# Pooled attention and two MLPs on one core: block 1's attention steps two intervals later, keys of heads 5 to 7 pooled on VectorE, the last product token tile by token tile

## The chip, the core and the metric

One NeuronCore of a Trainium2 chip runs the whole program. The metric is device time in microseconds (us) of one launch. The engines are TensorE (PE, with its weight loads PEld), VectorE (DVE), ScalarE (ACT), GpSimd (POOL) and SyncE (SP), whose queue issues nearly all DMAs. Each engine takes its instructions strictly in the order in which the program wrote them and waits on semaphores for the others, so an instruction that waits holds up everything behind it on its engine.

## The reference

```python
def _attn_ref(q, k, v):            # 8 x 8 heads, 576 tokens, head_dim 64
    k_p = k.reshape(B, H, 72, 8, D).mean(axis=3)     # keys and values pooled by 8
    v_p = v.reshape(B, H, 72, 8, D).mean(axis=3)
    scores = scale * np.matmul(q, k_p.transpose(0, 1, 3, 2))
    attn = softmax(scores)
    return np.matmul(attn, v_p)
...
x = attn_out.transpose(0, 2, 1, 3).reshape(4608, 512)
h = x @ w_in;  x = (h * clip(h + 3, 0, 6) / 6) @ w_out           # MLP 1, d_ff 2048
g = x @ w_gate;  out = (silu(g) * (x @ w_val)) @ w_out2           # MLP 2, d_ff 1536
```

The weights arrive as float64 words and are turned into float32 on the chip. All products are made to float32 accuracy from two halves (a high part and a rest), so each product is three matmuls.

## The kernel before

**Attention.** The 4608 tokens are cut into 9 blocks of 512. Heads are taken in pairs ("head" in the code is such a pair; heads 0 to 3 are batch 0, 4 to 7 batch 1). A *unit* is a piece of one head pair's tokens: block 0 has units 0 to 7, block 1 units 8 to 19. Each unit goes through steps with one-letter names: S (scores on PE, then the row maximum on DVE, L453 and L459), X (exponentials on ACT, L476), N (reciprocal of the row sum on DVE, L491 and L492), M (scaling on POOL, L496), E (split of a tail, L503 and L506), T (transposes on PE, L513 and L517), U and L (copy and rest of the transposed tile, ACT L526, DVE L533), V (product with the values on PE, L539 to L542), W and Y (result into the tile x, ACT L550, DVE L554). For each head there are steps for keys (RK and K) and values (R0, R1, R), and for each segment of queries a step P, which on DVE is the transposition L440 of a loaded tile q_in.

**The order.** Two tables, `when_startup` for the units of block 0 and `when` for all others, give each step of unit i an interval (i plus a lag) and a rank in it; all steps are sorted by these into one list. The steps up to the last Y of block 0 run before any MLP work. The rest of the list is dealt out evenly over the MLP's loop, counted by the large steps S, T and V, so that block j+1's attention runs beside block j's MLP 1.

**Keys.** Step RK sums 8 keys per row on DVE (`reduce_k`, two reductions L370), and K then transposes the sum on PE with one matmul (L389). For heads in `pe_pooled` there is no RK: K lets PE add the 8 rows with 16 small matmuls (L393), which the profile shows as 32.

**MLP 1 in block 0.** For each of 16 slices f there is a product h (12 matmuls, L561, needs all of x), an activation (ACT L583, DVE L585), a split, and two slices later a product y (12 matmuls). In block 0 the same loop also turns the weights from float64 into float32, two tiles per f: load into a buffer wstg (3 buffers, L108 on SP), rescale (ACT L120), join (DVE L126, L129), high part (ACT L169), rest (DVE L177). Six such conversions are steps C of the startup. The load of a new tile waits on SP for the join that frees its buffer.

**MLP 2** runs in 6 passes after the last block; its last part, `down2` with n = 6, makes three token tiles of 128 rows in three PSUM banks, chunk by chunk over the inner dimension, and `evac` adds them to the output tile o12 (DVE) and stores it.

The key step, the point where the two ways part:

```python
if what == "RK":
    if i not in pe_pooled:
        reduce_k(*heads[i])
        next_k(i)
elif what == "K":
    transpose_k(*heads[i])
```

Of the kernel before, what the change touches and what calls it, by code (L numbers as in the profile page):

```python
# [12 lines left out]
ALU = mybir.AluOpType  # L13
# [10 lines left out]
def kernel(  # L24
# [27 lines left out]
    nc = tc.nc  # L52
    P = 128
# [34 lines left out]
    M = 384  # L88
    NG = NT // (2 * M)
    NPAIR = F2 // 2  # L90
    PT = M // P
# [489 lines left out]
    def act1(ps):  # L581
        t = t_p.tile([P, N], F32, tag="t", name="t")
        nc.scalar.activation(out=t, in_=ps, func=ACTF.Relu, bias=three)  # L583
        g = t_p.tile([P, N], F32, tag="g32", name="g32")
        nc.vector.scalar_tensor_tensor(out=g, in0=t, scalar=6.0, in1=ps, op0=ALU.min, op1=ALU.mult)  # L585
        return g
# [27 lines left out]
    CH = 2  # L614
    l2 = {}
    xc, ys, gf, gc, wr = {}, {}, {}, {}, {}
# [46 lines left out]
    def bank():  # L663
        return l2["ps"].tile([P, 512], F32, tag="b", name="b")

    def mm3x(ps, w, x, first, last):
        for n, (wh, xh) in enumerate(((0, 0), (0, 1), (1, 0))):
            nc.tensor.matmul(out=ps, lhsT=w(wh), rhs=x(xh), start=first and n == 0, stop=last and n == 2)  # L668
# [4 lines left out]
    def up2(p, u):  # L673


        f, m = u
        add = lambda dst, a, b: nc.vector.tensor_tensor(out=dst, in0=a, in1=b, op=ALU.add)  # L677
        for what, wa, xb in UP:
            b = bank()[:, :M]
            w, x = wr.pop(("up", u, A7[wa])), xc[p, xb]  # L680
            for k in range(2):
                mm3x(b, lambda a: w[:, a, k], lambda a: x[:, a, k], k == 0, k == 1)
            if what == "P1":
                c11 = tmp(f"c11{m}")
                nc.scalar.copy(out=c11, in_=b)  # L685
            elif what == "P6":
                c21 = tmp(f"c21{m}")
                add(c21, c11, b)
            elif what == "P5":
                c12 = tmp(f"c12{m}")  # L690
                add(c12, c21, b)
            elif what == "P2":
                add(c11, c11, b)
            elif what == "P4":
                add(c21, c21, b)
            elif what == "P7":
                c22 = tmp(f"c22{m}")
                add(c22, c12, b)
                add(c21, c21, b)
            else:  # L700
                add(c12, c12, b)
        return {"11": c11, "22": c22, "21": c21, "12": c12}
# [6 lines left out]
    def gate2(c):  # L709
        g = {}  # L710
        for q in ("11", "22", "21", "12"):
            g[q] = tmp("s" + q)
            nc.scalar.activation(out=g[q], in_=c[q], func=ACTF.Sigmoid)  # L713
        for q in ("11", "22", "21", "12"):
            nc.gpsimd.tensor_tensor(out=g[q], in0=g[q], in1=c[q], op=ALU.mult)  # L715
        return g
# [18 lines left out]
    def down2(p, n):  # L735
        what = DN[n][0]
        b = dn_b[what] = [bank()[:, :2 * P] for i in range(PT)]
        for c in range(NPAIR // CH):
            g = gc.pop((p, n, c))
            for t in range(PT):  # L740
                for k in range(CH):
                    w = wr["dn", n, CH * c + k]
                    mm3x(b[t], lambda a: g[:, a, k, t * P:(t + 1) * P], lambda a: w[:, a],
                         c == 0 and k == 0, c == NPAIR // CH - 1 and k == CH - 1)

    o_t = {}

    def evac(p, n):

        what = DN[n][0]  # L750
        b = dn_b[what]

        def out_tile(tag):
            o_t[tag] = l2["o"].tile([P, PT, 2 * P], F32, tag=tag, name=tag)
            return o_t[tag]

        def add(dst, a):
            for t in range(PT):
                nc.vector.tensor_tensor(out=dst[:, t], in0=a[:, t], in1=b[t], op=ALU.add)

        def copy(dst):
            for t in range(PT):
                nc.scalar.copy(out=dst[:, t], in_=b[t])

        def store(tag, r, c):
            t0 = 2 * M * p + M * r
            nc.sync.dma_start(
                out=out[t0:t0 + M, 2 * P * c:2 * P * (c + 1)].rearrange("(t p) d -> p t d", p=P),
                in_=o_t[tag],
            )  # L770

        if what == "P1":
            copy(out_tile("o12"))
        elif what == "P4":
            copy(out_tile("o21"))
        elif what == "P2":
            add(out_tile("o11"), o_t["o12"])
            store("o11", 0, 0)
        elif what == "P6":
            add(o_t["o12"], o_t["o12"])  # L780
            nc.vector.tensor_tensor(out=o_t["o21"], in0=o_t["o21"], in1=o_t["o12"], op=ALU.add)
        elif what == "P5":
            add(o_t["o12"], o_t["o12"])
        elif what == "P7":
            add(o_t["o21"], o_t["o21"])
            add(out_tile("o22"), o_t["o12"])
            store("o21", 1, 0)
            store("o22", 1, 1)
        else:
            add(o_t["o12"], o_t["o12"])  # L790
            store("o12", 0, 1)

# [8 lines left out]
    for j in range(NB):  # L801
        t0 = j * N
        while t0 < (j + 1) * N:
            b, s0 = t0 // S, t0 % S
            n = min(S - s0, (j + 1) * N - t0)
# [14 lines left out]
        unit_end.append(len(units))  # L820
    NU = len(units)
    early_units = set(units[:unit_end[1]])
    pe_pooled = {5, 6, 7}

# [15 lines left out]
    }  # L840
    events = []
    for i in range(NU):
        startup_unit = i < unit_end[0]
        lag = dict(when_startup if startup_unit else when)
        if 0 <= i - unit_end[0] < NE:
            lag["E"] = (1, 22)
        stages = [(what, i) for what in "SXNMETULVWY"]
        if 2 <= i < 8:
            stages.append(("C", i))
        if i in first_in_seg:  # L850
            stages.append(("P", first_in_seg[i]))
        if i in first_in_head:
            stages += [(what, first_in_head[i]) for what in ("RK", "K", "R0", "R1", "R")]
        events += [(i + lag[st[0]][0], lag[st[0]][1], st[1], st) for st in stages]
# [119 lines left out]
    with tc.manual_schedule():  # L974
# [6 lines left out]
            out=vmask[:, 0], in_=vmask[:, 0], compare_op=ALU.is_ge, fill=0.0,  # L981
# [3 lines left out]
            out=vmask[:, 1], in_=vmask[:, 1], compare_op=ALU.is_ge, fill=0.0,  # L985
# [45 lines left out]
        for n, (j, f) in enumerate(seq1):  # L1031
# [13 lines left out]
            g = act1(hp)  # L1045
# [28 lines left out]
        for p in range(NG):  # L1074
            for n, (f, m) in enumerate(units2):
                c = up2(p, (f, m))
                load_next()
                if m == 0:
                    g = gate2(c)
                else:  # L1080
                    val2(p, f, g, c)
                    if f % CH == CH - 1:
                        split_gc(p, 0, f // CH, nc.vector)
                        split_gc(p, 1, f // CH, nc.vector)
                        if f + 1 < NPAIR:
                            sums_g(p, ("S1", "S3", "S2"), f + 1 - CH, f + 1)
                if n == 2 and p + 1 < NG:
                    load_y(p + 1, y_pool)
            NC = NPAIR // CH
            for n in range(7):  # L1090
                down2(p, n)
                load_next()
                if n + 2 < 7:
                    for c in range(NC):
                        split_gc(p, n + 2, c, nc.vector)
                if n == 0:
                    sums_g(p, ("S1", "S3", "S2"), NPAIR - CH, NPAIR)
                    for a in range(0, NPAIR, NPAIR // 2):
                        sums_g(p, ("S4",), a, a + NPAIR // 2)
                evac(p, n)  # L1100
                if p + 1 < NG:
                    x_step(p + 1, n, nc.vector, nc.vector)
# [29 lines left out]
```

## Time and profile before

| what | value |
|---|---|
| median of 3 runs | 1784.87 us (1782.77 to 1784.95) |
| profiled execution | 1784.89 us, span of its instructions 1783.1 us |
| mean granted TensorE clock | 0.989 of full speed |
| PE busy | 1741.5 us (98%) |
| DVE, ACT, POOL busy | 1208.7 us, 687.5 us, 632.7 us |

The span is the time from the first to the last instruction; 1.8 us of the execution lie around it. Times in the trace count from the span's start. A granted clock of 1.00 is the higher of TensorE's two levels (2.4 GHz), 0.50 the lower (1.2 GHz). A row of a timeline gives start, length, engine, line, operation, output and input, and in brackets how long the engine had been idle and what ended that.

### The profile page before, as it was taken

How to read it: one execution, taken by the hardware profiler on the slowest of the kernel's cores; microseconds unless marked ns; L12 is line 12 of the kernel's file. 1: busy time of each engine (PE TensorE's matmuls, PEld its weight loads, DVE VectorE, ACT ScalarE, POOL GpSimd, SP SyncE). 2: the span in 40 equal slices, each digit the busy share in tenths (PEclk: the TensorE clock that was granted, in tenths of full speed). 3: DMA queues.
4: the chain of work that ended last, by engine and by line, in shares of the span. 5: the costliest groups of instructions: out<-in, count | busy, mean ns of one | idle time of the engine just before them, and what ended most of it. 6: DMA issues, size and time to landing. Idle time of an engine off the chain costs nothing.

```text
span 1783.1 us, 28056 instructions
## 1 busy us (share of the span) xinstructions
PE 1741.5 (98%) x9945; PEld 1575.7 (88%) x9945; DVE 1208.7 (68%) x2216; ACT 687.5 (39%) x1580; POOL 632.7 (35%) x769
## 2 busy tenths in 40 slices
PE   5899999999999999999999999999999999999999
PEld 4677788888888878878888999999999999999999
DVE  7887677768577666765522468568668568668666
ACT  6565444434444434444323225124224224224222
POOL 5343342414315133251112351361461460550550
PEclk8899999999999999999999999999999999999999
DMA  7765557666657666565354677977977877878776
GB/s 173 224 221 168 177 166 243 211 203 194 206 182 208 219 187 203 169 182 197 113 207 179 238 255 249 329 249 255 328 246 258 316 247 269 314 245 279 272 245 213
DMA packets 196315, 402.93 MB, mean 226 GB/s; under 512 B 85840, under 2 KB 121680, under 8 KB 185424
## 3 DMA queue, kind: packets, MB, share of 16 engines
q1 hardware_dynamic: 192528, 396.16, 67.8%
q10 hardware_dynamic: 3648, 4.98, 0.8%
q8 instruction: 79, 1.29, 0.3%
q14 instruction: 60, 0.49, 0.1%
HBM read 340.79 MB, written 60.29 MB: 225 GB/s over the span
## 4 chain that ended last, share of the span: by engine, by line
PE 89%; DVE 4%; ACT 2%; DMA 2%; issue 1%; POOL 1%; SPq 0%; DVEq 0%; POOLq 0%; ACTq 0%
PE b L668 44%; PE y L561 20%; PE h L561 19%; PE pss L453 2%; PE pst L513 1%; PE pst L517 1%; DMA qs<-in_q_dram 1%; DVE fly L177 1%; ACT e L476 1%; DVE w L129 1%; DVE w L126 1%; PE psv L542 1%; DMA vts<-in_v_dram 1%; PE psv L540 0%; PE psv L541 0%
## 5 line engine op out<-in xcount | busy, mean ns | idle before, releaser
L668 PE MATMUL b<-xc,wr 128*128 128x384 f32 x3024 | 525.2, 334 | 0.0
L668 PEld LDWEIGHTS b<-xc,wr 128*128 128x128 f32 x3024 | 524.0, 188 | 0.1
L561 PE MATMUL y<-g,fly 128*128 128x512 f32 x1728 | 431.8, 399 | 1.6 <-ACT yo L602 1.6
L561 PE MATMUL h<-x,wu 128*128 128x512 f32 x1728 | 431.9, 399 | 0.0
L677 DVE TENSOR_TENSOR c<-c,b 128x384 f32<-128x384 f32 x504 | 265.0, 552 | 178.6 <-PE b L668 151.4
L561 PEld LDWEIGHTS y<-g,fly 128*128 128x128 f32 x1728 | 319.4, 190 | 66.3 <-ACT yo L602 2.0
L561 PEld LDWEIGHTS h<-x,wu 128*128 128x128 f32 x1728 | 319.4, 190 | 64.4 <-issue 0.4
L715 POOL TENSOR_TENSOR s<-s,c 128x384 f32<-128x384 f32 x144 | 142.5, 1015 | 400.4 <-ACT s L713 400.4
L668 PE MATMUL b<-wr,gc 128*128 128x256 f32 x2268 | 265.6, 279 | 0.0
L668 PEld LDWEIGHTS b<-wr,gc 128*128 128x128 f32 x2268 | 265.4, 188 | 0.0
L496 POOL TENSOR_TENSOR e<-e,sm 96x288 f32<-96x288 f32 (+3 forms) x85 | 70.5, 830 | 466.4 <-DVE sm L492 331.0
L722 POOL TENSOR_TENSOR gf<-s,c 128x384 f32<-128x384 f32 x144 | 168.3, 1194 | 67.0 <-DVE c L677 66.2
L134 ACT CAST gc<-gf 128x768 fp32r<-128x768 f32 x126 | 105.6, 838 | 187.0 <-POOL gf L722 99.8
L713 ACT ACTIVATE s<-c 128x384 f32<-128x384 f32 x144 | 73.5, 526 | 202.4 <-DVE c L677 201.2
L135 DVE TENSOR_TENSOR gc<-gf,gc 128x768 fp32r<-128x768 f32 x126 | 133.7, 1093 | 15.7 <-ACT gc L134 13.9
L135 DVE TENSOR_TENSOR g<-g,g 128x512 fp32r<-128x512 f32 x128 | 93.9, 733 | 67.4 <-ACT g L134 66.8
L585 DVE SCALAR_TENSOR_TENSOR g<-t,h 128x512 f32<-128x512 f32 x144 | 97.6, 678 | 60.4 <-ACT t L583 57.0
L134 ACT CAST g<-g 128x512 fp32r<-128x512 f32 x144 | 88.7, 616 | 68.5 <-PE y L561 47.6
L583 ACT ACTIVATE t<-h,three 128x512 f32<-128x512 f32 x144 | 98.5, 684 | 38.9 <-PE h L561 38.5
L483 ACT ACTIVATE e<-e 96x288 f32<-96x288 f32 (+3 forms) x76 | 31.4, 413 | 153.2 <-DVE e L480 151.5
L685 ACT COPY c<-b 128x384 f32<-128x384 f32 x72 | 34.0, 472 | 144.9 <-PE b L668 144.9
L205 DVE TENSOR_TENSOR gf<-gf 128x768 f32<-128x768 f32 (+1 forms) x66 | 66.9, 1029 | 12.2 <-POOL gf L722 10.9
(105 smaller groups left out, 1635.3 us busy)
## 6 DMA issues: line engine op xcount, KB each, us to landing
wr<-sup SPq DMA_DIRECT2D x72, 1024.0 KB
fly<-w1d SPq DMA_DIRECT2D x128, 512.0 KB
wr<-sdn SPq DMA_DIRECT2D x84, 768.0 KB
wr<-sup SPq DMA_DIRECT2D x72, 768.0 KB
sup<-s SPq DMA_DIRECT2D x12, 1792.0 KB
sdn<-s SPq DMA_DIRECT2D x6, 1792.0 KB
ystg<-y SPq DMA_DIRECT2D x24, 384.0 KB
out_dram<-o SPq DMA_DIRECT2D x24, 384.0 KB
```

The costliest lines, as they stand in the source:

```text
L134: nc.scalar.copy(out=hi, in_=src)
L135: lo_engine.tensor_tensor(out=lo, in0=src, in1=f32(hi), op=ALU.subtract)
L205: eng.tensor_tensor(out=v(what), in0=v(a), in1=v(b), op=op)
L496: nc.gpsimd.tensor_tensor(out=e3, in0=e3, in1=sm.to_broadcast(list(e3.shape)), op=ALU.mult)
L561: nc.tensor.matmul(out=ps, lhsT=w(kt, wh), rhs=x(kt, xh), start=first and n == 0, stop=last and n == 3 * len(kts) - 1,)
L583: nc.scalar.activation(out=t, in_=ps, func=ACTF.Relu, bias=three)
L585: nc.vector.scalar_tensor_tensor(out=g, in0=t, scalar=6.0, in1=ps, op0=ALU.min, op1=ALU.mult)
L668: nc.tensor.matmul(out=ps, lhsT=w(wh), rhs=x(xh), start=first and n == 0, stop=last and n == 2)
L677: add = lambda dst, a, b: nc.vector.tensor_tensor(out=dst, in0=a, in1=b, op=ALU.add)
L713: nc.scalar.activation(out=g[q], in_=c[q], func=ACTF.Sigmoid)
L715: nc.gpsimd.tensor_tensor(out=g[q], in0=g[q], in1=c[q], op=ALU.mult)
L722: nc.gpsimd.tensor_tensor(out=gf[p][:, GP[TURN[q]], f], in0=g[q], in1=c[q], op=ALU.mult)
```

## The change

Three edits. `HOLD = 2` adds two intervals to every step of units 8 and up, while block 0's units stay; since all later units move alike, only their order against the startup changes. `pe_pooled` is emptied, so heads 5, 6 and 7 get the step RK on DVE and the short K on PE like all others. In the last pass the last product runs token tile by token tile, and each tile is added and stored as it is done.

```diff
     def down2(p, n):
...
+        order = [(c, t) for c in range(NC) for t in range(PT)]
+        if (p, n) == (NG - 1, 6):
+
+            order.sort(key=lambda ct: ct[1])
+        for c, t in order:
+            g = gc[p, n, c]
...
-            add(o_t["o12"], o_t["o12"])
-            store("o12", 0, 1)
+            for t in range(PT):
+                o = o_t["o12"][:, t]
+                nc.vector.tensor_tensor(out=o, in0=o, in1=b[t], op=ALU.add)
+                if p == NG - 1:
+                    t0 = 2 * M * p + P * t
+                    nc.sync.dma_start(out=out[t0:t0 + P, 2 * P:], in_=o)
+            if p < NG - 1:
+                store("o12", 0, 1)
...
-    pe_pooled = {5, 6, 7}
+    pe_pooled = set()
...
+    HOLD = 2
...
+        if not startup_unit:
+            lag = {what: (a + HOLD, rank) for what, (a, rank) in lag.items()}
```

What this does to the order shows at three places. On PE, the first product h before; the steps ahead of it are units 6 to 8's transposes, unit 10's scores (`kbd_130`), then the value products of unit 8 (64 columns) and unit 7 (256 columns):

```order
L513 MATMUL pst<-ident,es 128x64
L517 MATMUL pst<-ident,et_142 96x64
L453 MATMUL pss<-kbd_130,qT 64x144
L539 MATMUL psv<-aT,vst_132 128x64
L540 MATMUL psv<-aT,vst_132 128x64
L541 MATMUL psv<-aT,vst_132 128x64
L542 MATMUL psv<-aTt,vtl_136 128x64
L539 MATMUL psv<-aT,vst_135 128x256
L540 MATMUL psv<-aT,vst_135 128x256
L541 MATMUL psv<-aT,vst_135 128x256
L542 MATMUL psv<-aTt,vtl_139 128x256
L561 MATMUL h<-x,wu 128x512 x12
```

The same place of the change:

```order
L453 MATMUL pss<-kbd_128,qT 64x144
L539 MATMUL psv<-aT,vst_135 128x256
L540 MATMUL psv<-aT,vst_135 128x256
L541 MATMUL psv<-aT,vst_135 128x256
L542 MATMUL psv<-aTt,vtl_139 128x256
L561 MATMUL h<-x,wu 128x512 x12
L453 MATMUL pss<-kbd_129,qT 64x144
L513 MATMUL pst<-ident,es 128x64
L517 MATMUL pst<-ident,et_142 96x64
L453 MATMUL pss<-kbd_130,qT 64x144
```

Scores of units 9 and 10 and transposes and value product of unit 8 have moved behind the first h; only unit 8's scores stay ahead of it. From the scores of unit 20 on, PE's order is the same in both.

On SP, the loads of the startup's last intervals before: the fourth and fifth weight tile (L108), values, and between them the queries of segments 6 and 7 (L361, four pieces each):

```order
L108 DMA wstg<-in_moe_w_in_dram 128x4x256
L361 DMA q_in<-in_q_dram 32x2x32 x4
L108 DMA wstg<-in_moe_w_out_dram 128x1024
L314 DMA vts<-in_v_dram 16x512 x3
L308 DMA v_in<-in_v_dram 72x512
L309 DMA v_in<-in_v_dram 56x512
L308 DMA v_in<-in_v_dram 72x512
L309 DMA v_in<-in_v_dram 56x512
L361 DMA q_in<-in_q_dram 32x2x32 x4
L108 DMA wstg<-in_moe_w_in_dram 128x4x256
```

The same place of the change:

```order
L108 DMA wstg<-in_moe_w_in_dram 128x4x256
L108 DMA wstg<-in_moe_w_out_dram 128x1024
L314 DMA vts<-in_v_dram 16x512 x3
L308 DMA v_in<-in_v_dram 72x512
L309 DMA v_in<-in_v_dram 56x512
L308 DMA v_in<-in_v_dram 72x512
L309 DMA v_in<-in_v_dram 56x512
L108 DMA wstg<-in_moe_w_in_dram 128x4x256
L108 DMA wstg<-in_moe_w_out_dram 128x1024
L361 DMA q_in<-in_q_dram 32x2x32 x8
```

The queries of segments 6 and 7 now stand behind the sixth and the seventh weight tile.

On DVE, the stretch between the scores' maxima of units 12 and 13 in the change, where head 5's reduction comes in:

```order
L585 SCALAR_TENSOR_TENSOR g_940<-t,h 128x512
L126 TENSOR_SCALAR w_944<-wstg 128x512
L129 SCALAR_TENSOR_TENSOR w_944<-wstg,w_944 128x512
L177 TENSOR_TENSOR fly<-w_902,fly 128x512
L554 TENSOR_TENSOR x<-psv,x 128x64
L370 TENSOR_REDUCE kp<-k_in 72x64 x2
L126 TENSOR_SCALAR w_985<-wstg 128x512
L129 SCALAR_TENSOR_TENSOR w_985<-wstg,w_985 128x512
L177 TENSOR_TENSOR wu<-w_944,wu 128x512
L533 TENSOR_TENSOR aT<-pst,aT 128x64
L459 TENSOR_REDUCE mx<-pss 96x4
```

The pair L370 is new here, and again once each for heads 6 and 7; before, DVE went from L554 to the conversion at once.

## Rows read from the trace of the kernel before

**Rows 1.** Busy time by stretch: start:end, length, engines, granted clock, DMA share, GB/s.

```profile
50.00:168.00 118.00, 108.79 (x564) 88.22 (x564) 97.93 (x181) 71.94 (x216) 49.33 (x60) 0.94 0.69 210
...
168.00:187.00 19.00, 19.00 (x94) 15.83 (x93) 10.62 (x22) 5.67 (x15) 3.51 (x5) 1.00 0.55 160
```

The columns after the length are PE, PEld, DVE, ACT and POOL.

**Rows 2.** The chain that ended last, stretch 50 to 168, by line.

```profile
by line: issue 10.2%; PE h L561 9.8%; ACT e L476 9.0%; DVE fly L177 8.5%; DVE w L129 7.6%; DVE w L126 7.4%; PE y L561 6.4%; PE psk L393 6.3%; DVE wu L177 5.7%; DVE g L585 4.8%; ACT t L583 3.0%; DVE mx L459 2.9%; ACT wstg L120 1.6%; DVE aT L
```

**Rows 3.** Timeline of DVE, end of startup and first slice.

```profile
45.33 0.24 DVE L440 STREAM_TRANSPOSE qT<-q_in 128x64 f32<-128x64 f32 x1 [1.80 <-DMA q_in<-in_q_dram]
...
46.17 0.80 DVE L129 SCALAR_TENSOR_TENSOR w<-wstg,w 128x512 int32<-128x512 int32 x1
...
47.83 0.21 DVE L533 TENSOR_TENSOR aT<-pst,aT 128x64 fp32r<-128x64 f32 x1
...
48.05 0.29 DVE L459 TENSOR_REDUCE mx<-pss 64x2 f32<-64x144 f32 x1
...
48.68 0.65 DVE L440 STREAM_TRANSPOSE qT<-q_in 128x448 f32<-128x448 f32 x1
...
51.24 0.54 DVE L554 TENSOR_TENSOR x<-psv,x 128x256 fp32r<-128x256 f32 x2
...
55.16 0.23 DVE L533 TENSOR_TENSOR aT<-pst,aT 128x64 fp32r<-128x64 f32 x1 [1.47 <-ACT aTt L527]
...
56.37 0.16 DVE L491 TENSOR_SCALAR sm<-sm 64x2 f32<-64x2 f32 x1 [0.78 <-ACT e L476]
```

**Rows 4.** Timeline of SP's queue: the issue of segment 7's four query pieces.

```profile
41.40 1.73 SPq L361 DMA_DIRECT2D q_in<-in_q_dram  x4
```

**Rows 5.** Timeline of PE: first product, key matmuls of heads 5 to 7, products behind.

```profile
49.75 4.75 PE L561 MATMUL h<-x,wu 128*128 128x512 f32 x12
...
77.24 3.40 PE L393 MATMUL psk<-ident,k_in 72*64 72x72 f32 x32 [3.32 <-ACT e L476]
80.57 4.79 PE L561 MATMUL h<-x,wu 128*128 128x512 f32 x12
...
88.80 3.00 PE L561 MATMUL h<-x,wu 128*128 128x512 f32 x12
...
100.16 2.02 PE L393 MATMUL psk<-ident,k_in 72*64 72x72 f32 x32 [0.69 <-ACT e L476]
...
123.05 2.02 PE L393 MATMUL psk<-ident,k_in 72*64 72x72 f32 x32 [1.47 <-ACT e L476]
125.00 4.62 PE L561 MATMUL y<-g,fly 128*128 128x512 f32 x12
```

**Rows 6.** All reductions L370 on keys: ns min/median/max of one.

```profile
L370 DVE TENSOR_REDUCE kp<-k_in x50: 1024/1067/1116, 51.7 to 764.5; 72x64 f32<-72x512 f32 x50
```

**Rows 7.** Timeline of DVE: four waits inside block 0.

```profile
86.51 0.42 DVE L533 TENSOR_TENSOR aT<-pst,aT 128x256 fp32r<-128x256 f32 x1 [2.13 <-ACT aTt L527]
...
130.31 0.69 DVE L177 TENSOR_TENSOR fly<-w,fly 128x512 fp32r<-128x512 f32 x1 [1.12 <-ACT fly L169]
131.40 0.42 DVE L533 TENSOR_TENSOR aT<-pst,aT 128x256 fp32r<-128x256 f32 x1 [0.40 <-ACT aTt L527]
...
138.91 0.69 DVE L585 SCALAR_TENSOR_TENSOR g<-t,h 128x512 f32<-128x512 f32 x1 [1.43 <-ACT t L583]
```

**Rows 8.** DVE by line and shape, 50 to 168: busy us, mean ns.

```profile
L129 DVE SCALAR_TENSOR_TENSOR w<-wstg,w 128x512 int32<-128x512 int32 x28 | 27.2, 972 | 1.0
L177 DVE TENSOR_TENSOR wu<-w,wu 128x512 fp32r<-128x512 f32 x14 | 15.3, 1090 | 0.0
```

**Rows 9.** Line L129 alone, same stretch: ns min/median/max.

```profile
L129 DVE SCALAR_TENSOR_TENSOR w<-wstg,w x28: 691/695/2275, 49.9 to 162.3; 128x512 int32<-128x512 int32 x28
```

**Rows 10.** Timeline of DVE: the last instruction.

```profile
1779.27 0.42 DVE L759 TENSOR_TENSOR o<-o,b 128x256 f32<-128x256 f32 x1 [0.28 <-PE b L668]
```

**Rows 11.** Busy time by stretch, the end (last columns DMA share, GB/s).

```profile
1780.00:1781.00 1.00, 0.00 (x0) 0.00 (x0) 0.00 (x0) 0.00 (x0) 0.00 (x0) 1.00 0.36 125
1781.00:1782.00 1.00, 0.00 (x0) 0.00 (x0) 0.00 (x0) 0.00 (x0) 0.00 (x0) 1.00 0.78 268
```

More of the change, by code (lines that the diff above doesn't have):

```diff
@@ L737, in down2 @@
         b = dn_b[what] = [bank()[:, :2 * P] for i in range(PT)]
[L738 to L744, printed above, removed]
+        NC = NPAIR // CH
+        order = [(c, t) for c in range(NC) for t in range(PT)]
[3 more added lines that the diff above has]
+            g = gc[p, n, c]
+            for k in range(CH):
+                w = wr["dn", n, CH * c + k]
+                mm3x(b[t], lambda a: g[:, a, k, t * P:(t + 1) * P], lambda a: w[:, a],
+                     c == 0 and k == 0, c == NC - 1 and k == CH - 1)
     o_t = {}
```

## The prediction

> **What bounds the kernel now.** I first read busy time by stretch. Between 168 and 187 us PE is busy for all 19.00 us [rows 1], and over the whole run its busy share is 98%: from block 1 on, PE alone sets the time. None of the three edits takes PE work out of that part, except at the very end. So the change is decided before about 168 us and in the last microseconds. In block 0's stretch, 50 to 168, PE is busy 108.8 of 118 us and DVE 97.9 [rows 1], and busy time doesn't say which of them sets the pace. The chain that ended last does: its steps there are mostly DVE and ACT rows (conversion L126, L129, L177; exponentials L476; activation L585), h and y of PE together are 16%, and L393 is 6.3%, which is 7.4 us [rows 2]. DVE's idle time is made of short waits for ACT and PE. So block 0 runs at DVE's pace, with PE on the path for moments, above all where PE pools a key: 3.40, 2.02 and 2.02 us, each behind a wait for the exponentials, and twice the product behind it ran at about half speed (4.79 and 4.62 us against 3.00) [rows 5].
>
> That gives the method: the three edits are counted on DVE's queue, from the last startup row (L554 of unit 7, which ends near 51.6 us, first of two at 51.24 [rows 3]) to the end of block 0, and every us there is taken to move block 1, and so the end, by one us.
>
> **The hold, in the startup.** DVE loses the rows of units 9 and 10 and one of unit 8 ahead of unit 7's L554: a transposition L440 of 0.24 us and one of 0.65, two L459 of 0.29, one L533 of 0.21 [rows 3], and five short rows (L491, L492, L506) of about 0.16 as the L491 at 56.37 [rows 3]: together 2.3 to 2.4 us. Their order shows that 1.4 us of these stood ahead of the join of the fourth weight tile. The 1.80 us for which L440 waited for its queries [rows 3] goes too. So that join, which ended at 46.17 + 0.80 = 46.97, now ends near 46.97 - 1.80 - 1.4 = 43.8 us.
>
> But the wait comes back at another place. Segment 6's queries now stand on SP behind the seventh weight tile, whose load waits for the buffer that just this join frees. From there: one issue, 1.73 / 4 = 0.4 us [rows 4], four query pieces, 1.73 us [rows 4], and the landing, which took 45.33 - 41.40 - 1.73 = 2.2 us [rows 3, 4]: the queries are there at 48.1 us. Before, the way from that join to the next L440 took 48.68 - 46.97 = 1.7 us [rows 3], of which one L533 (0.21) is gone; DVE is at the L440 at 45.3 us and stands there for 2.8 us instead of 1.8. From the L440 to the end of the L533 behind it went 48.04 - 45.33 = 2.7 us [rows 3], and about the same rows now lead to unit 7's L554: it ends at 50.8 us against 51.6. **Startup: -0.8 us.** Bounds: if the queries land without any wait, -3.7; if the 512 KB weight tile issued just ahead delays them by a further 2 us (more than any wait of this kind in the rows), +1.2.
>
> PE starts its first h near 46 us instead of 49.75 [rows 5], but the last three matmuls need unit 7's part of x, so it stops and ends not far before 52 us. That lead is worth nothing while DVE is behind.
>
> **The hold, in block 0.** The 2.4 us of DVE rows come back here: **+2.4**. Scores of unit 9 now follow the first h on PE; DVE, free at 50.8, waits until about 52.4 (three matmuls at the lower clock, 4.75 / 4 = 1.2 us [rows 5], and two small ones). Then come the waits of L491 for the exponentials of units 9 and 10, 0.78 each as at 56.37 [rows 3]. That is 1.6 + 1.6 = 3.2 us, against 1.47 + 0.78 = 2.25 in the same place before [rows 3]: **+0.9**.
>
> **The keys.** Three pairs of L370 on DVE, at no less than 1.02 us each [rows 6], 6 x 1.02 = **+6.1**. They stand ahead of conversions, not in a wait, so nothing covers them. In exchange PE's 7.4 us of L393 shrink to three single matmuls. What of that reaches DVE is only what DVE waited for PE behind those places: 2.13 us after the first key, 1.12 + 0.40 after the third, nothing after the second [rows 7]: **-3.6**. Bounds: 0, if PE is late again, and -7.4, if all of L393 was on the path.
>
> The Trainium skill (VectorE: DVE Perf Modes, sections on the TRN2 errata and Rules for kernel authors) speaks against such a reduction: it calls tensor_reduce the slowest VectorE operation. Its cycle table would make one of 512 elements (58 + 512) / 0.96 GHz = 0.59 us, an estimate; with it the keys would cost 3.6 us and the sum below would end 2.5 us lower, at 1784.4. Rows 6 have no row under 1.02 us, so the measurement decides.
>
> **Two side effects.** The 1.43 us wait of L585 at 138.91 [rows 7] came from an order of steps (reciprocal, L554, then at once L585) which in the changed order has a conversion between: **-1.4**, bounds 0 and -1.4. And DVE and POOL hinder one another: L129 took 0.69 us at its shortest but 0.97 in the mean of 28 and 2.28 once [rows 8, 9], 28 x 0.28 = 7.9 us lost on this line alone; L177 on wu has a mean of 1.09. The reductions L370 are hardly ever stretched (1.02 to 1.12 over 50 [rows 6]), so POOL can work beside them. DVE gains 6.1 us of such time and loses about 4.1 us of waits (3.6 + 1.4 - 0.9) in which POOL was also free; POOL is busy 49.3 / 118 = 42% [rows 1]: 2.0 x 0.42 = **-0.8**. Which POOL rows meet which DVE rows is new after every shift, so I take bounds of -3.5 and +2.5.
>
> **The tail.** The last add starts at 1779.27 [rows 10]; then 384 KB go out between about 1780.6 and 1781.8 [rows 11]: 0.36 + 0.78 = 1.1 us of all DMA engines. With one tile in three left, 2/3 of that, 0.76 us, goes: **-0.8**. The two earlier stores and the new order of matmuls cost nothing, being hidden under the remaining products.
>
> **The sum.** -0.8 + 2.4 + 0.9 + 6.1 - 3.6 - 1.4 - 0.8 - 0.8 = +2.0 us. The profiled execution took 1784.9 us (the median is the same), so 1786.9 us.
>
> **The rivals.** A change of 0.2% is 3.6 us, about what a measurement of this kernel can tell from none: the limits are 1781.3 and 1788.4.
>
> *Forecast*: DVE sets block 0, and what PE gives back and what DVE takes on nearly cancel: 1786.9 us, by itself 1783 to 1788.4. Chance 0.46.
>
> *PE sets block 0 (faster).* Then L393 (7.4 us) and the two slow products (1.79 + 1.62 = 3.4 us) [rows 5] come off the time, with the tail 11.6 us: 1773.3 us. For it: PE is busy 92% there and L393 stands on the chain. Against it: DVE's rows make up most of that chain, and PE's waits before L393 are for exponentials that come from a late DVE row. It decides below 1781.3 when at least a third of the 10.8 us on PE arrives in place of the +2.8 that the sum has without the tail; a mix with a startup without wait ends near 1779. Chance 0.20.
>
> *The keys' waits stay (slower).* PE, with less to do, comes to each key earlier and stands longer: before the first the wait was 3.32 us, and it was after such a pause that h took 4.79 us, at 1.2 GHz [rows 5]. If the clock falls behind all three keys, the transposes behind those products are late again and DVE gets none of the 3.6 + 1.4 us back: 1786.9 + 5.0 = 1791.9 us. It decides as soon as 1.5 us of these 5.0 stay away. For it: the chain runs through e, L393, h to DVE's L533 today. Against it: between the key and that L533 DVE now has its own rows for about 6 us. Chance 0.30, with the part of the contention bounds that goes the same way.
>
> *Nothing but the tail shows*: the hold and the keys cancel fully, 1784.1 us. That is inside "same", chance 0.04.
>
> **How the numbers follow.** Predicted is the likeliest case, 1786.9 us. Low 1780.5 takes in the mixed faster case near the limit, high 1791.9 is the slower rival; outside are the full PE case and a startup delay on top of the slower one, about 0.2 together. Faster 0.20, same 0.50, slower 0.30.
>
> **What would show it.** First h near 46 us with a hole before its last three matmuls; a wait of L440 for queries of 2.5 to 3 us near 45 to 48 us; unit 7's L554 ending within 1 us of 51; three pairs of L370 of 2.0 us; the waits of L533 behind the keys gone; PE's waits before the keys longer than 3.32, 0.69 and 1.47 us, with PE's busy time in block 0 some 10 us lower; the first product of block 1 some 3 us later; 128 KB in the last transfer. I am wrong if DVE isn't idle less often in block 0 than before, if the chain there turns to PE, or if POOL's share in stretched L126, L129 and L177 rows changes by more than 3 us.

## The result and the profile after

| | before | after |
|---|---|---|
| median of 6 runs, us | 1784.84 (1782.77 to 1785.52) | 1794.9 (1792.64 to 1797.49) |
| ratio to before | | 1.0061, 95% interval 1.0049 to 1.0072 |
| span of the profiled execution, us | 1783.1 | 1790.9 |

The change makes the kernel slower, by 0.61% in the ratio (10 us in the medians, 7.8 us between the two profiled executions). Forecast were 1786.9 us and a range up to 1791.9. The profile of before is one of its slower executions (1784.9 us, where those measured beside the experiments lie between 1780.1 and 1786.0 us), so differences between profiles come out up to 2 us smaller than the medians say.

First, busy time by stretch, to be held against [rows 1]; the columns are the same.

```profile
50.00:168.00 118.00, 96.39 (x427) 76.04 (x427) 98.77 (x187) 69.85 (x218) 48.64 (x61) 0.91 0.67 202
168.00:187.00 19.00, 19.00 (x94) 15.82 (x93) 11.81 (x26) 6.58 (x16) 5.37 (x6) 1.00 0.42 129
```

PE has 12.4 us less busy time in the same 118 us, DVE 0.8 more, and block 0 isn't over at 168. How much later it is over is read from one row: the L554 of unit 17, for which PE's scores of the next unit wait (1.77 us before; 3.06 us after, at 160.79 in the PE rows below). Behind it PE has only short waits in block 0. Here is the row, of before and of after:

```profile
151.21 0.34 DVE L554 TENSOR_TENSOR x<-psv,x 128x192 fp32r<-128x192 f32 x1
```

```profile
160.39 0.34 DVE L554 TENSOR_TENSOR x<-psv,x 128x192 fp32r<-128x192 f32 x1
```

It ended at 151.55 before and at 160.73 after, 9.2 us later. From there to the end took 1631.6 us before and 1630.2 after. So the time went into the stretch from unit 7's L554 (before, unit 8's stands right behind it and is counted with it) to unit 17's. Here it is whole, first of before, then of after.

```profile
51.78:151.55 99.77, 91.16 (x485) 74.11 (x484) 80.82 (x145) 63.31 (x195) 44.07 (x53) 0.94 0.70 214
```

```profile
52.37:160.73 108.36, 87.97 (x396) 69.58 (x396) 89.61 (x165) 65.99 (x207) 45.35 (x55) 0.92 0.69 207
```

DVE's busy time grew from 80.82 to 89.61 us, and its idle time, length less busy, is 18.95 and 18.75 us: the same. The start is 0.6 us later. That is the whole ledger: +0.6 + 8.8 - 0.2 = +9.2 us.

The idle time is the same in sum only. Cut in two at the row maximum of unit 12 (L459, at 64.58 before and at 80.41 after), the stretch reads, of before and of after:

```profile
51.78:64.58 12.80, 12.20 (x56) 9.29 (x56) 10.19 (x22) 7.20 (x21) 1.71 (x2) 0.93 0.73 210
64.58:151.55 86.97, 78.96 (x430) 64.81 (x429) 70.63 (x125) 56.12 (x174) 42.36 (x51) 0.94 0.69 215
```

```profile
52.37:80.41 28.04, 20.43 (x79) 15.28 (x80) 20.61 (x43) 14.29 (x43) 6.46 (x7) 0.82 0.75 206
80.41:160.73 80.32, 67.54 (x319) 54.30 (x317) 69.00 (x124) 51.70 (x164) 38.90 (x48) 0.95 0.67 207
```

In the first slices DVE is idle 7.4 us instead of 2.6 (+4.8), and behind them 11.3 instead of 16.3 (-5.0). What DVE waited for in the two whole stretches (total us, times, longest), first before:

```profile
DVE sm L491 <- ACT e L476: 9.7, 9, 1.4
DVE aT L533 <- ACT aTt L527: 4.0, 3, 2.1
DVE g L585 <- ACT t L583: 2.4, 5, 1.4
DVE fly L177 <- ACT fly L169: 1.1, 1, 1.1
```

and after:

```profile
DVE sm L491 <- ACT e L476: 10.6, 11, 1.4
DVE g L585 <- ACT t L583: 1.9, 6, 0.5
DVE fly L177 <- ACT fly L169: 1.7, 1, 1.7
DVE et L506 <- ACT et L503: 1.5, 2, 0.8
DVE mx L459 <- PE pss L453: 1.2, 1, 1.2
```

The waits of L533 are gone, behind the keys as forecast, and others stand in their place (a row of 0.3 us each at the ends of the lists is left out). DVE's timeline of after shows where:

```profile
49.78 0.25 DVE L440 STREAM_TRANSPOSE qT<-q_in 128x64 f32<-128x64 f32 x1 [3.83 <-DMA q_in<-in_q_dram]
51.96 0.41 DVE L554 TENSOR_TENSOR x<-psv,x 128x256 fp32r<-128x256 f32 x1
53.59 0.30 DVE L459 TENSOR_REDUCE mx<-pss 64x2 f32<-64x144 f32 x1 [1.21 <-PE pss L453]
...
54.66 0.16 DVE L491 TENSOR_SCALAR sm<-sm 64x2 f32<-64x2 f32 x1 [0.62 <-ACT e L476]
...
55.86 0.17 DVE L506 TENSOR_TENSOR et<-e,et 64x16 f32<-64x16 f32 x1 [0.73 <-ACT et L503]
56.45 0.69 DVE L585 SCALAR_TENSOR_TENSOR g<-t,h 128x512 f32<-128x512 f32 x1 [0.42 <-ACT t L583]
...
59.79 0.16 DVE L491 TENSOR_SCALAR sm<-sm 64x2 f32<-64x2 f32 x1 [0.23 <-ACT e L476]
...
63.24 1.94 DVE L370 TENSOR_REDUCE kp<-k_in 72x64 f32<-72x512 f32 x2
...
66.75 1.76 DVE L177 TENSOR_TENSOR fly<-w,fly 128x512 fp32r<-128x512 f32 x1
68.44 0.21 DVE L533 TENSOR_TENSOR aT<-pst,aT 128x64 fp32r<-128x64 f32 x1
...
71.30 0.16 DVE L491 TENSOR_SCALAR sm<-sm 64x2 f32<-64x2 f32 x1 [0.78 <-ACT e L476]
...
72.52 0.17 DVE L506 TENSOR_TENSOR et<-e,et 64x16 f32<-64x16 f32 x1 [0.75 <-ACT et L503]
73.23 0.69 DVE L585 SCALAR_TENSOR_TENSOR g<-t,h 128x512 f32<-128x512 f32 x1 [0.55 <-ACT t L583]
...
76.73 0.69 DVE L177 TENSOR_TENSOR fly<-w,fly 128x512 fp32r<-128x512 f32 x1 [1.75 <-ACT fly L169]
```

and PE's, for the same slices and the later keys:

```profile
46.80 4.41 PE L561 MATMUL h<-x,wu 128*128 128x512 f32 x10
52.43 0.73 PE L561 MATMUL h<-x,wu 128*128 128x512 f32 x2 [1.22 <-DVE x L554]
...
68.70 0.42 PE L539 MATMUL psv<-aT,vst 128*128 128x64 f32 x1 [4.88 <-DVE aT L533]
...
71.32 0.38 PE L389 MATMUL psk<-ident,kp 72*128 72x72 f32 x1 [1.55 <-ACT e L476]
71.44 4.60 PE L561 MATMUL y<-g,fly 128*128 128x512 f32 x12
...
91.56 0.28 PE L389 MATMUL psk<-ident,kp 72*128 72x72 f32 x1 [1.07 <-ACT e L476]
91.65 4.58 PE L561 MATMUL h<-x,wu 128*128 128x512 f32 x12
...
113.46 0.28 PE L389 MATMUL psk<-ident,kp 72*128 72x72 f32 x1 [2.31 <-ACT e L476]
...
160.79 0.85 PE L453 MATMUL pss<-kbd,qT 128*128 128x144 f32 x2 [3.06 <-DVE x L554]
```

Unit 9's value product stands 4.88 us because its L533 is at 68.44, behind the key reductions of head 4, L585 and a conversion. PE then waits again, 1.55 us ahead of head 4's key, and the y behind it takes 4.60 us against some 3.0, at a granted clock of 0.62 in the mean of 71.44 to 75.97. ACT's high part of a weight tile waits for this y to free its buffer, and DVE's rest of that tile (L177 at 76.73) waits for ACT:

```profile
76.08 0.62 ACT L169 CAST fly<-w 128x512 fp32r<-128x512 f32 x1 [2.88 <-PE y L561]
```

At the end the new order shows as intended. The last add:

```profile
1787.77 0.42 DVE L796 TENSOR_TENSOR o<-o,b 128x256 f32<-128x256 f32 x1 [1.68 <-PE b L668]
```

From its end to the end of the span are 2.7 us, before it were 3.4 (1783.1 - 1779.69, [rows 10]): 0.7 us less.

### The profile page after: what moved, and what is told of

It reads as the page before. It is cut to its first block, busy times and chain, and to the rows that moved or that the text cites. A ratio compares the mean times of both kernels' runs of the same rounds, so it can differ in the third digit from the quotient of the medians.

```text
span 1790.9 us, 27879 instructions
## 1 busy us (share of the span) xinstructions
PE 1738.9 (97%) x9852; PEld 1571.8 (88%) x9852; DVE 1214.0 (68%) x2222; ACT 687.0 (38%) x1580; POOL 633.1 (35%) x769
## 4 chain that ended last, share of the span: by engine, by line
PE 87%; DVE 5%; DMA 3%; ACT 2%; issue 1%; SPq 1%; POOL 1%; DVEq 0%; POOLq 0%; ACTq 0%
PE b L668 44%; PE y L561 19%; PE h L561 19%; PE pss L453 2%; DVE kp L370 1%; DMA y<-yo 1%; PE pst L513 1%; DVE w L129 1%; PE pst L517 1%; ACT e L476 1%; DMA fly<-w1d 1%; DMA vts<-in_v_dram 1%; DVE fly L177 0%; PE psv L542 0%; DVE w L126 0%
## 5 line engine op out<-in xcount | busy, mean ns | idle before, releaser
L496 POOL TENSOR_TENSOR e<-e,sm 96x288 f32<-96x288 f32 (+3 forms) x87 | 71.4, 821 | 471.7 <-DVE sm L492 340.3
L135 DVE TENSOR_TENSOR gc<-gf,gc 128x768 fp32r<-128x768 f32 x126 | 133.8, 1093 | 15.6 <-ACT gc L134 13.9
L135 DVE TENSOR_TENSOR g<-g,g 128x512 fp32r<-128x512 f32 x128 | 94.3, 737 | 68.1 <-ACT g L134 67.5
L585 DVE SCALAR_TENSOR_TENSOR g<-t,h 128x512 f32<-128x512 f32 x144 | 97.6, 678 | 59.1 <-ACT t L583 56.0
L205 DVE TENSOR_TENSOR gf<-gf 128x768 f32<-128x768 f32 (+1 forms) x66 | 66.9, 1029 | 12.2 <-POOL gf L722 10.9
```

The costliest lines, as they stand in the source:

```text
L135: lo_engine.tensor_tensor(out=lo, in0=src, in1=f32(hi), op=ALU.subtract)
L205: eng.tensor_tensor(out=v(what), in0=v(a), in1=v(b), op=op)
L496: nc.gpsimd.tensor_tensor(out=e3, in0=e3, in1=sm.to_broadcast(list(e3.shape)), op=ALU.mult)
```

## The experiments

In the kernels below a time is compared with runs of before on the same chip; a difference in us is taken from the ratio.

**One part of the change at a time.** The hold alone:

```
+            lag = {what: (a + HOLD, rank) for what, (a, rank) in lag.items()}
```

> Only the units of block 1's tokens held back by two intervals; keys and last product as before. Theory D (VectorE's queue up to unit 17's last row of block 0 sets the time; what TensorE is spared returns only as waits that other waits replace): about +0.7 us of later startup, +2.5 of moved rows, +1.8 of one conversion more ahead of unit 17, with some waits more: +4 to +7 us. Rival S (the hold and its late queries are nearly all of the +10): +8 to +10. Rival K (the keys are nearly all): -1 to +2.

Measured, with `HOLD = 2`: 1789.05 us, ratio 1.0033 (1.0020 to 1.0045), +5.9 us: theory D's side.

The keys alone (`pe_pooled = set()`):

> Only the keys of heads 5 to 7 pooled on VectorE. Theory D: six reductions put 6.1 us on VectorE, the waits behind TensorE's key sums (2.13, 1.12, 0.40 us) and the 1.43 go as far as they are not replaced: +1 to +4 us. Rival P (TensorE sets block 0): 7.4 us of key sums and 3.4 us of half-speed products come off: -7 to -10. Rival S: 0. Rival K: +6 to +9.

Measured: 1786.01 us, ratio 1.0016 (1.0007 to 1.0024), +2.9 us: theory D again; rivals P, S and K lie outside the interval.

The last product alone (order of `down2`, adds and stores by tile):

> Only the last product token tile by token tile. All theories: -0.5 to -0.9 us, since the last transfer shrinks from 384 to 128 KB, and nothing else moves.

Measured: 1784.2 us, ratio 1.0006 (0.9997 to 1.0015). The 0.7 us that the rows show at the end aren't resolved by the times. The hold makes more than half of the loss; the parts sum to 5.9 + 2.9 + 1.1 = 9.9 us (8.1 with the -0.7 of the rows for the tail), near the 10.9 of the ratio. Each part is known to about 2 us only, so the times don't tell whether they add up exactly.

This kernel differs from before in its last product alone, so its profile is a second one of the same block 0: unit 7's L554 ends at 53.15 us there (51.78 before) and unit 17's at 151.34 (151.55). What differs by less than some 1.5 us between two profiles below is therefore not resolved.

**Keys on both engines, and on neither.** On both: heads 5 to 7 stay on PE, and DVE adds them up as well.

```
+                for h2, t in enumerate(k_t[heads[i]]):
+                    nc.vector.tensor_reduce(out=kp[:, h2], in_=t.rearrange("s o d -> s d o"), axis=AX.X, op=ALU.add)
```

> Kernel before, where TensorE still pools the keys of heads 5 to 7 and VectorE adds them up too (six reductions more, whose sum nobody reads): TensorE is spared nothing, VectorE is loaded as in the change. Theory D: 6.1 us less what of the waits for TensorE (3.6 us) the reductions fill: +3 to +6. Rival P (TensorE sets block 0, VectorE has room): 0 to +1. The run against the one with the keys alone gives what sparing TensorE is worth: by D 0 to 3 us, by P 7 to 10.

Measured: 1794.54 us, ratio 1.0066 (1.0053 to 1.0078), +11.8 us, beyond every expectation. PE's timeline of this kernel, against [rows 5]:

```profile
79.22 3.68 PE L393 MATMUL psk<-ident,k_in 72*64 72x72 f32 x32 [2.73 <-ACT e L476]
82.83 5.49 PE L561 MATMUL h<-x,wu 128*128 128x512 f32 x12
...
104.75 3.22 PE L393 MATMUL psk<-ident,k_in 72*64 72x72 f32 x32 [2.31 <-ACT e L476]
107.90 4.97 PE L561 MATMUL y<-g,fly 128*128 128x512 f32 x12
...
131.97 3.15 PE L393 MATMUL psk<-ident,k_in 72*64 72x72 f32 x32 [2.61 <-ACT e L476]
135.05 5.04 PE L561 MATMUL y<-g,fly 128*128 128x512 f32 x12
```

Behind all three waits the sums and the product run at a granted clock of 0.50 to 0.60 in the mean: 10.4 us over 3 x 2.02 + 3 x 3.02, where before had 4.8 (two of three keys). DVE waits for that: its idle time is 23.89 us (table below). On neither:

```
-                for o in range(POOL):
+                for o in range(1):
```

> Kernel before with the keys of heads 5 to 7 pooled by nobody: TensorE takes only the first of the eight rows (one matmul of eight each), VectorE adds nothing. Left out is the sum over the other seven rows. The run with both engines pooling (+11.5 us) against the one with the keys on VectorE alone (+3.0) says that sparing TensorE is worth 8.5 us. Theory L (VectorE, ScalarE and TensorE take turns on one path through block 0, so TensorE's key sums and the half-speed products behind them count nearly in full): -6 to -9 us. Theory D (only VectorE's queue counts, TensorE's part returns as the waits of 3.6 + 1.4 us at most): -2 to -5.

Measured: 1781.59 us, ratio 0.9987 (0.9978 to 0.9996), -2.3 us, theory D's size. Together the two runs say that one engine's part can't be priced without the other's: sparing PE is worth 2.3 us when DVE has no reductions and 11.8 - 2.9 = 8.9 us when it has them.

**Size of the hold, and its queries.** `HOLD = 1`:

> Hold by one interval instead of two, nothing else changed. The hold by two alone cost 6.0 us. Theory Q (the late queries and the longer startup): most of it comes at the step at which the queries of segment 6 fall behind the seventh weight tile, so 0 to +1 us or nearly the whole +5 to +6, no middle. Theory F (the attention's chain from scores to value product starts empty in block 0 and must be run through there): about half, +2.5 to +4.

Measured: 1787.5 us (1780.9 to 1789.8, a wide spread), ratio 1.0017 (1.0006 to 1.0029), +3.0 (1.1 to 5.2): the mean is theory F's half, but two of the ten executions took about 1781 us and the other eight 1785.7 to 1789.8, and in the profiled one (1788.36 us) unit 17's L554 ended at 155.09, as late as with the hold by two (154.99). So a half isn't shown, and this run doesn't decide against theory Q.

The changed kernel with the queries' loads issued earlier:

```
-                    later.append((done[0] + 12, lambda n=n: load_q(segs[n], sync4)))
+                    later.append((done[0] + 2, lambda n=n: load_q(segs[n], sync4)))
```

> The changed kernel with the loads of the queries issued two steps after the segment is transposed, not twelve. Theory Q: the wait of 3.83 us for the queries shrinks below 2, unit 7's last row comes 2 to 3 us earlier and the time falls by as much, to 1790 to 1792 us. Theory F: the first slices of block 0 wait for the exponentials and TensorE's value product anyway: within 1 us of the changed kernel (1794.9).

Measured: 1794.63 us, ratio to before 1.0062 (1.0049 to 1.0075), the same as the changed kernel. The wait for the queries shrank to 2.43 us and unit 7's L554 ended 0.86 us earlier, but nothing of it is left at 76 us. PE's rows:

```profile
67.89 0.42 PE L539 MATMUL psv<-aT,vst 128*128 128x64 f32 x1 [3.68 <-DVE aT L533]
...
70.63 5.47 PE L561 MATMUL y<-g,fly 128*128 128x512 f32 x12
```

This y starts 0.8 us earlier than at 71.44 above and ends at the same time (76.1 and 76.0), since it spends longer at the lower clock (granted 0.50 against 0.62 in the mean). Theory F holds; the wait didn't go below 2 us as theory Q had it, but what came back of it was worth nothing here.

**One head more on PE**, with the tail (`pe_pooled = {4, 5, 6, 7}`):

> Kernel before with the last product token tile by token tile and with the keys of head 4 pooled on TensorE too (VectorE pools none of block 1's keys). Moving three heads the other way cost 3.0 us, so theory L: -1.0 us for the head and -0.7 for the tail, -1 to -2. Theory D: 2.0 us off VectorE and nothing lost, -2 to -3.5. Rival P (TensorE sets it): +1 to +3.

Measured: 1785.64 us (1780.16 to 1789.72), ratio 1.0011 (1.0001 to 1.0022), +2.0 (0.2 to 3.9): rival P's side, against theories L and D. Head 4's reductions lie in a wait of DVE in the kernel before: they stand between the L554 at 51.24 and the L533 at 55.16, which waits another 1.47 us behind them [rows 3]. So taking them off DVE should give little back, and PE pays for the sums. Its profile doesn't show the loss, though: in that execution (1783.85 us, the eleven reach from 1780.2 to 1789.7) unit 17's L554 ended at 149.97, 1.6 us earlier than before. Where the +2.0 comes from stays open.

**PE's key work one product later.** If standing PE is the cost, let products run in the waits:

```
+        if first_in_head.get(i) in (5, 6, 7):
+            lag["K"] = (0, 17)
```

> Kernel before, with TensorE's sums for heads 5, 6 and 7 placed one product and one transposition later in its order (behind the step T of the unit, not ahead of it); the same rows on every engine otherwise. In the profile of before TensorE stands 3.32, 0.69 and 1.47 us ahead of these sums for the exponentials, and 4.8 us are lost to half speed behind two of them. Theory T (TensorE's standing still and its half speed behind it are the time of block 0): the products run in these waits and the time falls by 4 to 9 us. Theory D (VectorE's queue sets it): within 1.5 us of before.

Measured: 1788.46 us, ratio 1.0032 (1.0022 to 1.0041), +5.7: slower, and both theories fall, T in this form and D because DVE has the same rows and yet the time moved. The wait didn't go, it changed its releaser:

```profile
83.41 3.68 PE L393 MATMUL psk<-ident,k_in 72*64 72x72 f32 x32 [4.50 <-DVE x L554]
```

Scores, transposes, value products and keys take turns on two PSUM tiles (the ring "att"). Placed one step later the key gets the tile of the value product, which DVE's L554 must empty first, and stands longer than before; DVE's idle time rises to 23.70 us (table below). The same edit on the other two kernels:

> Keys of heads 5 to 7 on VectorE (+3.0 us by itself), with the transposition of these keys on TensorE one product later. Its waits ahead of that were 2.73, 2.29 and 2.91 us, and four products behind a wait lost 1.6 to 2.5 us each at half speed. Theory T: 6 to 10 us less than the keys alone, so 3 to 7 us faster than before. Theory D: +2 to +4 us as the keys alone, since VectorE has the same rows.

> The changed kernel, with the transposition of the keys of heads 4 to 7 one product later. Its waits there were 1.55, 1.07, 2.31 and 1.21 us. Theory T: 4 to 8 us less than the changed kernel (+10), so +2 to +6. Theory D: within 1.5 us of the changed kernel.

Measured: 1787.35 us, ratio 1.0022 (1.0013 to 1.0031), and 1795.67 us, 1.0066 (1.0054 to 1.0079). Neither gained, as theory D has it for both.

**Matmuls in the waits.** Unread matmuls into the tile that the next h product overwrites, ahead of the key (heads 5 and 7; in the second kernel 5, 6 and 7):

```
+                for _ in range(fill[i]):
+                    nc.tensor.matmul(out=nxt[0], lhsT=w, rhs=x, start=True, stop=True)
             transpose_k(*heads[i])
```

> Kernel before, where TensorE runs 8 matmuls whose result nobody reads (2.0 us at full speed) in its wait of 3.32 us ahead of the key sums of head 5, and 4 (1.0 us) in the wait of 1.47 us ahead of those of head 7, so that it stands for 1.3 and 0.5 us only; 4.8 us were lost at half speed behind these two waits. Theory H (a wait costs twice, once as standing and once as half speed behind it): the half speed goes, 2 to 5 us faster than before. Rival (half speed there is hidden behind VectorE): within 1 us.

Measured: 1781.24 us, ratio 0.9986 (0.9977 to 0.9995), 2.5 us faster than before, theory H's size and the best kernel of this study that leaves nothing out. No key of heads 5 to 7 and no product behind one runs at the lower clock any more (granted 1.00 from 77.22 to 82.16 and from 120.15 to 125.10, where before had 0.55 to 0.62 in the sums of head 5 and in both products); only the first h of block 0 still does (4.74 us):

```profile
73.75 2.10 PE L926 MATMUL h<-x,wu 128*128 128x512 f32 x8
77.22 2.02 PE L393 MATMUL psk<-ident,k_in 72*64 72x72 f32 x32 [1.37 <-ACT e L476]
79.17 3.06 PE L561 MATMUL h<-x,wu 128*128 128x512 f32 x12
...
118.53 1.11 PE L926 MATMUL h<-x,wu 128*128 128x512 f32 x4
120.15 2.02 PE L393 MATMUL psk<-ident,k_in 72*64 72x72 f32 x32 [0.50 <-ACT e L476]
122.10 3.06 PE L561 MATMUL y<-g,fly 128*128 128x512 f32 x12
```

The wait ends where it did (77.22 against 77.24), what follows is faster.

> Keys of heads 5 to 7 on VectorE (+3.0 us by itself), with 8, 6 and 8 unread matmuls in TensorE's waits of 2.73, 2.29 and 2.91 us ahead of the three transpositions; 1.6 to 2.5 us were lost at half speed behind each. Theory H: 4 to 6 us faster than the keys alone, 1 to 3 us faster than before. Rival: within 1 us of the keys alone.

Measured: 1785.9 us, ratio 1.0009 (1.0000 to 1.0018); the keys alone had 1.0016 (1.0007 to 1.0024) in other runs, and the intervals overlap. Here the products behind the three keys take 3.01 us each (5.47, 4.58 and 4.58 in the keys alone), and unit 17's L554 ends where it did without the fill, at 152.27 against 152.28. So the lower clock costs time where PE pools the keys, and none that these runs resolve where DVE does: theory H falls there.

**The hold's cost taken apart.** Head 4's reductions left where they were (`lag["RK"] = when["RK"]` for that head):

> Hold by two intervals alone (+6.0 us), with one step left where it was: the two reductions L370 of head 4, which the hold moves from behind unit 7's last row (where they lie in a wait) to 63.4 us, ahead of the row for which TensorE stands 4.87 us. Theory M (a step that was hidden in a wait is now in front of work): they fill the wait of 1.21 us of L459 again, TensorE's 4.87 us shrink to about 3.5, and the time falls by 1 to 2.5 us against the hold. Rival (the hold costs through its waits for the exponentials alone): within 0.7 us of the hold.

Measured: 1791.0 us, ratio 1.0048 (1.0035 to 1.0060); no gain against the hold's 1.0033. The wait of L459 was filled and PE's wait fell by even more than expected, to 1.89 us, but the y behind it then took 5.33 us instead of 4.58, and DVE's L177 waited 2.49 us for it, by way of ACT, instead of 1.73. Theory M falls: its waits shrank as it said, and the time didn't follow. Whether the kernel lies within the rival's 0.7 us of the hold isn't resolved.

The hold with the keys of heads 5 to 7 pooled by nobody:

> Hold by two intervals, with the keys of heads 5 to 7 pooled by nobody (one of eight rows taken, the sum over the other seven left out). Without the hold, sparing TensorE these sums brought unit 17's last row forward by 3.9 us, from 151.55 to 147.64. Theory W (the hold has already taken away the waits which those sums cause, so that nothing is left to give back): that row stays within 1 us of the 154.99 of the hold, and the time within 1.5 us of 1789. Additive rival: it comes near 151, and the time is 3 to 4 us below the hold's.

Measured: 1790.99 us, ratio 1.0042 (1.0028 to 1.0056). Unit 17's row came at 157.30, no earlier than with the sums, though PE's busy time in the stretch fell by 3.4 us. The additive rival falls. Theory W's limits are missed too, on the later side (1 us for the row, 1.5 us around 1789 for the time): the startup ended 0.8 us later in this execution, and DVE waited 2.0 us instead of 1.2 for the first scores. DVE has no wait at L533 here, as it has none in the changed kernel.

The stretch from the end of unit 7's L554 to the end of unit 17's, in the profiles (us; idle is length less busy):

| kernel | starts | ends | DVE busy | DVE idle | PE busy |
|---|---|---|---|---|---|
| before | 51.78 | 151.55 | 80.82 | 18.95 | 91.16 |
| tail alone (same block 0) | 53.15 | 151.34 | 80.69 | 17.50 | 89.63 |
| before, PE's keys one product later | 53.15 | 158.06 | 81.21 | 23.70 | 95.03 |
| waits filled | 51.96 | 147.10 | 80.36 | 14.78 | 89.19 |
| keys on neither | 52.68 | 147.64 | 80.92 | 14.04 | 84.50 |
| keys on DVE | 52.60 | 152.28 | 85.01 | 14.67 | 86.38 |
| keys on DVE, waits filled | 52.52 | 152.27 | 85.14 | 14.61 | 88.19 |
| keys on both | 52.61 | 162.01 | 85.51 | 23.89 | 96.68 |
| hold | 52.52 | 154.99 | 83.75 | 18.72 | 89.64 |
| hold, sums on neither | 53.34 | 157.30 | 84.52 | 19.44 | 86.25 |
| changed kernel | 52.37 | 160.73 | 89.61 | 18.75 | 87.97 |

## Why the prediction was wrong

**What held.** Block 0 decides; three pairs of L370 take 2.03, 2.06 and 2.06 us; the first h starts at 46.80 with a hole before its last matmuls; the tail gives 0.7 us. The four waits that were to come back (2.13, 1.12, 0.40 and 1.43 us [rows 7]) are all gone: behind the first slices DVE is idle 5.0 us less, just the 3.6 + 1.4 of the sum (3.6 less than in the profile of the tail alone). For the keys alone the sum was right within what the runs resolve: +6.1 - 3.6 - 0.8 = +1.7 forecast, +2.9 (1.2 to 4.3) measured, and the table shows the exchange, DVE busy +4.2 and idle -4.3.

Up to unit 17's row the sum without the tail has +2.8 us, and measured are +9.2. The 6.4 us between them:

**The step that failed: "first-slice waits, +0.9".** It put 3.2 us of waits against 2.25; measured are +4.8 us of idle time (7.4 against 2.6). Up to unit 12's maximum the timeline of after has nine waits, 1.21 + 0.62 + 0.73 + 0.42 + 0.23 + 0.78 + 0.75 + 0.55 + 1.75 = 7.0 us, where before had 2.5 (1.47, 0.78 [rows 3] and one of 0.22). What the prediction counted, the scores and the exponentials of units 9 and 10, came out smaller than it said: 1.21 + 0.62 + 0.23 = 2.1 us. The other 5.0 us it put at nothing. It left out that each held unit hands over more often than that (the cast of et, the activation ahead of L585), and that unit 11 follows, whose 0.78 it subtracted with the waits of before and didn't add again. And it left out that PE, standing 4.88 us for a late L533, then runs y partly at the lower clock, for which DVE waits 1.75 by way of ACT. In the ledger the waits have -0.2 us instead of 0.9 - 3.6 - 1.4 = -4.1: this is 3.9 of the 6.4, and all of it lies in the first slices; the tail alone has the same 2.6 us there as before.

The hold does this by itself. Alone it has the same idle time as the changed kernel in both parts of the stretch: 7.4 us up to unit 12's maximum and 11.3 us behind it. So the waits behind the keys go with the hold alone, and the keys, put on top of it, find nothing to give back: from the hold to the changed kernel DVE's busy time rises by 5.9 us and its idle time by 0.0. The hold without the sums shows the same from PE's side. The sum counted these waits once, and rightly; but it priced them as the keys' gain, and in the change they are no longer that.

**The startup, -0.8, came out as +0.6**: 1.4 us more. L440 waited 3.83 us for its queries, not 2.8, and unit 7's L554 ended at 52.37. But ten profiles with the startup of before end it between 51.78 and 53.38, so this difference isn't resolved; against the profile of the tail alone it is -0.8. And in the run with earlier queries 0.86 us of it came back without any effect on the time: the rule that every us there moves the end by one doesn't hold for the startup.

**The rows, +2.4 + 6.1 - 0.8 = +7.7, came out as +8.8**: 1.1 us more. Up to unit 17's L554 there are 24 conversions instead of 23 (three rows, some 1.8 us), which the sum, counting moved attention rows alone, didn't have. The -0.8 for rows stretched beside POOL isn't resolved: a conversion's rows L126, L129 and L177 took 2.55 us in the mean before and 2.53 after.

The rival "the keys' waits stay" came nearest in time (1791.9 us), but by another mechanism: the DVE waits behind the keys did go, and PE's waits before the keys of heads 5 to 7, which this rival and the forecast both said would get longer, are 1.07, 2.31 and 1.21 us against 3.32, 0.69 and 1.47. With the keys alone its premise did come true (PE waits 2.73, 2.29 and 2.91 us, and the product behind each is slow), and still DVE got its waits back. The condition written down for being wrong, DVE not idle less often than before, is what happened.

What the whole study shows beyond the forecast: before, PE's sums and the lower clock behind them do set block 0 in part. With the waits filled, or the sums gone, DVE's idle time drops to 14 to 15 us and the row moves to 147. With keys on DVE it is 14.7 us at once, and filling PE's waits there moves nothing: DVE sets the pace.

Open: the hold measured +5.9 us (3.6 to 8.0), of which its profile shows 3.4 at unit 17's row. Which of the first slices' waits would have to go to make the hold free wasn't found; the two runs that took a piece away each had it given back by a slower y or a later wait.

## What to carry to other kernels

Work that is held back brings its hand-overs with it, and where it goes nothing may be left to run beneath them: count every wait of the moved chain, not only the moved rows. Take the busy and idle time of the engine that sets the pace from one named row to another, and cut the stretch at a third row; a subtraction then tells whether waits came back or only changed their place, and whether two edits live on the same ones. A second profile of the same code says which differences count. Where a wait can't be removed, what stands behind it may still be had: a few unread matmuls in PE's waits gave 2.5 us, while moving the waiting step only exchanged what it waited for.

## What the runs showed of the hardware

The lower clock came behind short waits already: in the changed kernel h took 4.58 us behind a wait of 1.07 us (granted clock 0.61 in the mean of 91.65 to 96.07). But not each time: y behind the wait of 2.31 us at 113.46 took 3.02 us at 1.00. The products that the prediction and the expectations call half speed have a granted clock of 0.59 and 0.62 in the kernel before (4.79 and 4.62 us [rows 5]): they run a part of their time at the lower level. With 2.10 us of matmuls in a wait of 3.32 us the next product took 3.06 us at 1.00.

DVE's reductions were hardly stretched beside POOL again: in the whole changed kernel the 56 rows of L370 took 0.99 to 1.11 us, while in the stretch above L129 took from 0.691 to 2.293 us with a median of 0.693. The Trainium skill (SBUF — State Buffer, section Who interferes with whom) says that tensor_reduce never contends with GpSimd on this chip, and that an operation with two SBUF inputs, as L129 is, does with GpSimd's reads; these rows agree. The longest L129, at 114.16, began while POOL was at work (L496 and L135, from 113.99 to 115.91).
